# One fused attention and expert kernel: scores of 64 queries as tiled float32 products, issued together with values

## The chip, the cores and the metric

The kernel runs on one core of one Trainium2 chip. The time is device microseconds from launch to end, as the median of some runs. Before the change three runs gave 751.17, 751.94 and 752.6 us, so the median is 751.94 us.

TensorE is called PE in the profile, VectorE DVE, ScalarE ACT, GpSimd POOL, and SyncE (here the engine that issues all loads and stores) SP.

## The reference

Input is q, k and v of 4 batches, 8 heads, 768 positions and 64 elements, and two weight matrices. Each query attends to its neighbours less than 16 positions away and to 24 summaries of 32 positions each; the summaries are a maximum over keys and a mean over values. Then a gated layer of width 2048 follows on the 3072 tokens of 512 elements.

```
k_sum = k.reshape(B, H, nb, block, D).max(axis=3)      # nb = 24, block = 32
v_sum = v.reshape(B, H, nb, block, D).mean(axis=3)
scores_l = scale * q @ k^T, kept where |i - j| < 16
scores_s = scale * q @ k_sum^T + log(32)
a = softmax over both; attn = a @ [v, v_sum]
h = x @ w_in;  g = h - tanh(h);  out = g @ w_out
```

## The kernel before

**Units.** The work is cut into 8 units `u`, each half of a batch's positions (384 queries) with all 8 heads. Attention of a unit goes by 4 pairs of heads `p` and 3 tiles of 128 queries `i`. The gated layer of a unit (called MoE in the code) goes by 16 steps `f`: products "in" into bank `pH`, activations, products "out" into the three banks `pY0` to `pY2`. The layer of unit u needs all four pairs of that unit, so attention of unit u+1 is run beside the layer of unit u, and only unit 0's attention stands alone at the start.

**Precision.** The first unit's layer takes whole float32 operands; the later ones take each operand as a high and a low part of a faster float32 kind (`F32R`) and add three products. The weights are read as raw words, and DVE and ACT turn each of the 32 weight tiles into numbers ("w scale", "w shift", "w low", "w sign"), later into a high and a low part.

**Scores before.** `prep` turns q and k with PE (`q turn`, `k turn`) and copies them out. k lies in a tile `[128, 2, KC]`: for each head of the pair its 64 rows, and zeros in the other 64. In units 0 and 1 (`u < WHOLE`) `scores` is one float32 product of 128 queries with 2 x 182 columns. From unit 2 on it is three `F32R` products with high and low parts, for which `prep` also makes `q low`, `q again`, `k low`, `k again`. 182 columns hold what 128 queries need; of these the first 64 queries use columns 0 to 117 and the last 64 use columns 64 to 181.

**Softmax before.** `softmax` works by tile. Because the two halves of 64 queries use other columns, `min` is run twice for each head, each on 64 partitions: it adds the mask and takes the minimum in one custom instruction, followed by a read of the accumulator. At the first and the last tile of a batch two memsets go before. Then per tile: two `exp` on ACT, `sum guard` and `inverse` on two sums, two `normal`. `transpose_probs` turns the probabilities with PE (`p turn`) and copies them out (`p out`), and `values` multiplies them with v: 12 float32 products for each pair, each of 64 columns into 64 partitions; in unit 0 they are issued tile by tile, from unit 1 on (`TOGETHER`) all 12 of a pair at once.

**Order.** Nothing runs in the order written. `plan.add` collects tasks with a cost in us, `Plan.schedule` chooses the task with the highest level at each moment, engine by engine, and the resulting order is what each engine executes, in order. `BIAS` adds to the level of single tasks, `KB` and `HALF` to that of a kind of task in one of three phases, `SL` says when an optional engine may take a task, and `keep_warm` fills PE's planned pauses before 100 us with products of the unit matrix (they appear as pX<-ident). All DMAs go through SP, in order, at most eight in flight.

Of the kernel before, what the change touches and what calls it, by code (L numbers as in the profile page):

```python
# [10 lines left out]
F32 = mybir.dt.float32  # L11
# [8 lines left out]
SLOTS = 4  # L20
# [7 lines left out]
TOGETHER = 1  # L28

WHOLE_IN = True  # L30
WHOLE_F = set(range(16))

WHOLE = 2

BIAS = {('top turn', 6): -62, ('p out', 19): -34, ('series', 46): -24, ('out', 95): 14, ('sum guard', 39): 21, ('p turn', 21): 39, ('q turn', 8): 13, ('square', 3): 43, ('w load', 29): 33, ('exp', 139): 10, ('x high', 7): 25, ('square', 16): -7, ('exp', 47): 33, ('square', 5): 41, ('series', 95): -20, ('in', 16): 12, ('square', 15): 11, ('w load', 26): 59, ('w load', 17): -20, ('values', 23): -12, ('w scale', 7): 30, ('sum guard', 45): 20, ('top turn', 4): 19, ('w load', 25): -45, ('w load', 23): 8, ('square', 13): 19, ('w sign', 2): 26, ('out', 13): -36, ('min', 142): 21, ('w load', 28): 24, ('series', 11): 5, ('normal', 25): -15, ('p out', 23): 32, ('pick', 8): 55, ('mean out', 3): 7, ('direct', 11): -29, ('w load', 15): -31, ('values', 20): 40, ('out', 14): -19, ('exp', 44): -17, ('square', 8): 4, ('w load', 27): 21, ('min', 39): 30, ('g', 9): -24, ('pick', 9): 4, ('inverse', 19): 36, ('direct', 8): -18, ('direct', 14): 20, ('q high', 8): 12, ('w high part', 21): -20, ('cube', 1): 21, ('normal', 44): -4, ('in', 8): 8, ('w sign', 10): -32, ('in', 1): 24, ('sum', 1): -20, ('x low', 7): -31, ('k load', 35): -9, ('tanh', 6): 20, ('v load', 39): -20, ('square', 9): 8, ('series', 15): -4, ('direct', 6): 1, ('v load', 90): 60, ('normal', 35): -15, ('values', 13): -30, ('exp', 37): -15, ('out', 58): 60, ('out', 67): -30, ('top put', 17): -5, ('k high', 3): 30, ('sum guard', 1): 60, ('top put', 80): 60, ('v load', 88): -45, ('g low', 56): -30, ('k load', 8): 60, ('k high', 36): -5, ('sum guard', 34): 15, ('out', 17): -5, ('mean put', 24): 5, ('sum guard', 2): -5, ('w low part 2', 22): -45, ('k again', 31): -15, ('k high', 12): -60, ('k load', 33): 30, ('inverse', 39): 5, ('min', 53): -15, ('tanh', 20): 30, ('out', 44): -30, ('y store', 23): 15, ('in', 13): 30, ('inverse', 88): -60, ('w low part 2', 24): 15, ('w sign', 18): 30, ('w low part 2', 4): -60, ('k high', 17): 60, ('k load', 37): 5, ('normal', 11): -15, ('chunk sum', 4): -60, ('top pre', 1): 60, ('top turn', 8): 30, ('x whole', 3): 5, ('scores', 37): 5, ('min', 165): 15, ('min', 23): 15, ('w shift', 6): 60, ('normal', 33): 30, ('w shift', 27): 60, ('w shift', 2): -30, ('chunk load', 11): 30, ('inverse', 4): -30, ('min', 46): -5, ('series', 9): -60, ('in', 21): 15, ('exp', 16): 15, ('normal', 70): -60, ('min', 6): -5, ('w low part 2', 20): -15, ('k turn', 4): 25, ('sum guard', 4): 60, ('q turn', 1): 30, ('out', 106): -5, ('in', 31): -5, ('g low', 96): 15, ('v load', 66): -5, ('top put', 52): -15, ('values', 9): 15, ('w high part 2', 29): -30, ('normal', 49): -30, ('chunk load', 3): 5, ('mean put', 11): 30, ('scores', 0): 30, ('g high', 26): -15, ('in', 30): 60, ('out', 38): -15, ('g high', 15): 60, ('q low', 3): -5, ('in', 12): 5, ('v load', 68): -60, ('w scale', 21): 15, ('p turn', 38): -45, ('out', 98): 15, ('k load', 25): 30, ('sum guard', 44): -30, ('g high', 99): -5, ('top put', 26): -30, ('w load', 4): 60, ('tanh', 71): -5, ('v load', 41): -5, ('w shift', 5): 30, ('v load', 141): 30, ('top put', 3): -5, ('q load', 8): 30, ('out', 89): -15, ('k load', 40): -30, ('v load', 43): 30, ('exp', 51): -60, ('w shift', 26): 5, ('scores', 34): 30, ('mean turn', 1): -30, ('out', 55): 5, ('w scale', 10): -30, ('tanh', 5): -60, ('exp', 30): -5, ('top put', 19): 5, ('out', 163): -60, ('v load', 21): -5, ('g low', 19): 5, ('g high', 86): -15, ('w shift', 7): 30, ('q low', 31): -60, ('g', 18): -5, ('x whole', 2): 15, ('w high part 2', 19): -5, ('q load', 19): -60, ('sum', 7): -30, ('min', 112): 30, ('v load', 89): 15, ('k load', 31): -5, ('tanh', 37): -15, ('inverse', 41): 30, ('out', 83): -15, ('w sign', 21): 30, ('k load', 3): -60}

PREP = [0, 2, 6, 11]

TOPS = {0: [(0, 0)], 1: [(0, 2)], 3: [(0, 1)], 5: [(0, 3)], 9: [(1, 3)], 11: [(1, 2)], 13: [(1, 0)], 15: [(1, 1)]}
SUMS = {0: [(0, 0)], 1: [(0, 1), (1, 1)], 8: [(0, 2)], 9: [(0, 3)], 10: [(1, 0)], 11: [(1, 2)], 13: [(1, 3)]}  # L40

# [1128 lines left out]
```

## Time and profile before

| | |
|---|---|
| median of three runs | 751.94 us |
| profiled execution, span from the first to the last instruction | 749.3 us |
| PE busy | 716.6 us (96%) |
| DVE busy | 479.4 us (64%) |
| ACT busy | 488.7 us (65%) |
| POOL busy | 225.7 us (30%) |
| mean granted PE clock | 0.993 |

The span is one profiled execution; the runs' times hold 2.6 us more (751.94 against 749.3) that lie outside its first and last instruction. A float32 product shows as two records in the profile, an `F32R` product as one; so 12 products of values show as x24. A matmul's record overlaps the next one's, so what a matmul costs is read from one start to the next, not from its duration. All helper calls share one line (L70), so groups are told apart by tile names: `pS` scores, `pT` turned things, `pX` values, `prob` probabilities, `probT` turned ones, `stat` minima and sums, `wraw` raw weights, `wf` and `wh` weights, `vw` values of v, `rawq` and `rawk` loaded q and k.

### The profile page before, as it was taken

The page shows a single profiled execution, that of the slowest core. Times are in us where ns is not written, and L with a number is a line of the kernel's source. Part 1 is how long each engine was busy: PE and PEld are TensorE (multiplying, and loading weights), DVE is VectorE, ACT ScalarE, POOL GpSimd, SP SyncE. Part 2 cuts the span into 40 slices and gives each one's busy share as a digit, 9 for nine tenths or more (in the row PEclk, how much of TensorE's full clock was granted, in tenths as well). Part 3 has the DMA queues.
Part 4 walks back from the last instruction along what each step waited for, and adds up shares of the span by engine and source line. Part 5 has one row for each costly group of instructions (what it writes and reads, how often), then busy time and mean ns, then how long its engine had stood idle before and what let it go on. Part 6 is the DMA issues. An engine that isn't in the chain of part 4 may idle for free. (4 is left out here: it accounts for less than half of the span.)

```text
span 749.3 us, 13632 instructions
## 1 busy us (share of the span) xinstructions
PE 716.6 (96%) x4351; PEld 590.2 (79%) x4351; DVE 479.4 (64%) x1685; ACT 488.7 (65%) x1413; POOL 225.7 (30%) x314
## 2 busy tenths in 40 slices
PE   7878899999999999999999999999999999999995
PEld 5655544457888898878888898889888888888994
DVE  5878999897775468774766558754767377651111
ACT  4557887648765577767777667656757577755442
POOL 3001221425434325453222225423132223222221
PEclk9989999999999999999999999999999999999999
DMA  9877586433031031423112131302112130101001
GB/s 234 234 216 187 173 229 194 164 101 91 30 82 23 17 86 65 103 72 95 44 30 54 39 87 54 83 5 77 45 25 58 39 87 1 40 1 43 1 1 48
DMA packets 121522, 61.03 MB, mean 81 GB/s; under 512 B 92512, under 2 KB 113248, under 8 KB 121440
## 3 DMA queue, kind: packets, MB, share of 16 engines
q1 hardware_dynamic: 121440, 60.06, 29.6%
q8 instruction: 37, 0.61, 0.3%
q14 instruction: 45, 0.37, 0.1%
HBM read 51.38 MB, written 6.29 MB: 77 GB/s over the span
## 5 line engine op out<-in xcount | busy, mean ns | idle before, releaser
L70 PE MATMUL pH<-xh,wf 128*128 128x384 f32 x548 | 186.5, 374 | 3.4 <-DVE wf L70 1.9
L70 POOL TENSOR_TENSOR gv<-gu,gt 128x384 f32<-128x384 f32 x109 | 111.5, 1024 | 236.1 <-DVE gl L70 142.8
L70 PE MATMUL pY<-wf,gh 128*128 128x512 f32 x432 | 178.6, 440 | 0.0
L70 PE MATMUL pH<-xh,wh 128*128 128x384 f32 x448 | 155.9, 348 | 0.0
L70 PE MATMUL pH<-xl,wh 128*128 128x384 f32 x448 | 152.2, 340 | 0.0
L70 PE MATMUL pY<-wh,gh 128*128 128x512 f32 x336 | 140.9, 419 | 0.0
L70 ACT ACTIVATE gu<-pH 128x384 f32<-128x384 f32 x128 | 62.5, 488 | 114.0 <-PE pH L70 95.9
L70 PE MATMUL pY<-wh,gl 128*128 128x512 f32 x336 | 132.0, 393 | 0.0
L70 ACT ACTIVATE prob<-prob,stat 128x118 f32<-128x118 f32 x236 | 92.0, 392 | 56.8 <-DVE stat L70 50.0
L70 PEld LDWEIGHTS pH<-xh,wf 128*128 128x128 f32 x548 | 102.4, 189 | 25.5 <-ACT gt L70 3.2
L70 DVE CUSTOM_DVE_ANT_0 prob<-pS,mask 64x118 f32<-64x118 f32 x352 | 98.0, 278 | 34.5 <-PE pT L70 15.3
L70 DVE TENSOR_TENSOR gl<-gv,gh 128x384 fp32r<-128x384 f32 x76 | 44.0, 579 | 90.4 <-ACT gh L70 83.7
L70 PEld LDWEIGHTS pY<-wf,gh 128*128 128x128 f32 x432 | 80.3, 189 | 20.8 <-issue 11.0
L70 PEld LDWEIGHTS pH<-xh,wh 128*128 128x128 f32 x448 | 84.5, 189 | 3.2 <-ACT prob L70 0.2
L70 PEld LDWEIGHTS pH<-xl,wh 128*128 128x128 f32 x448 | 83.9, 187 | 0.0
L70 PEld LDWEIGHTS pY<-wh,gl 128*128 128x128 f32 x336 | 63.1, 188 | 14.7
L70 PEld LDWEIGHTS pY<-wh,gh 128*128 128x128 f32 x336 | 63.4, 189 | 9.6
L70 ACT ACTIVATE gu<-gu 128x384 f32<-128x384 f32 x128 | 66.9, 523 | 0.2
L70 ACT ACTIVATE gt<-pH 128x384 f32<-128x384 f32 x128 | 61.8, 483 | 0.3
L70 POOL TENSOR_TENSOR gl<-gv,gh 128x384 fp32r<-128x384 f32 x36 | 37.6, 1045 | 78.7 <-ACT gh L70 36.3
L70 PE MATMUL pS<-k,q 128*128 128x364 f32 (+1 forms) x176 | 46.0, 343 | 8.3 <-DVE stat L70 5.1
L70 DVE TENSOR_SCALAR prob<-prob,stat 128x118 f32<-128x118 f32 x133 | 47.7, 385 | 2.4
(151 smaller groups left out, 1028.6 us busy)
## 6 DMA issues: line engine op xcount, KB each, us to landing
wraw<-in_moe_w_in_dram SPq DMA_DIRECT2D x16, 512.0 KB
wraw<-in_moe_w_out_dram SPq DMA_DIRECT2D x16, 512.0 KB
rawq<-in_q_dram SPq DMA_DIRECT2D x48, 128.0 KB
out_dram<-tmp SPq DMA_DIRECT2D x24, 256.0 KB
rawk<-in_k_dram SPq DMA_DIRECT2D x32, 128.0 KB
vw<-in_v_dram SPq DMA_DIRECT2D x40, 96.0 KB
vw<-in_v_dram SPq DMA_DIRECT2D x48, 64.0 KB
wraw<-in_k_dram SPq DMA_DIRECT2D x16, 192.0 KB
```

The costliest lines, as they stand in the source:

```text
L70: return lambda *args, **kwargs: self._tc.keep_in_program_order(op(*args, **kwargs))
```

## The change

**Scores.** q is now what gets the zeros: a tile `[128, 2, U]` in which head a has its 64 rows and zeros elsewhere, and k is a plain `[128, KC]` tile with both heads. A score product takes 64 queries of one head and the 118 columns that these need: 12 float32 products for each pair, in all units. The two halves of a tile go to different partitions (0 to 63 and 64 to 127) of the same columns of the bank, so that both use the same 118 columns. A pair's scores fill the two banks `pS0` and `pS1`. The low parts and second copies of q and k are gone.

**Together.** From unit 1 on the scores of a pair and the values of the pair before are one task (`scores_and_values`), so PE issues values and then scores without anything between.

**Softmax** is by pair: six `min` of 128 partitions, one for each tile and head, six `exp`, one guard and one inverse on six sums, six `normal`. The edge memsets became two further masks. `p turn` uses the banks `pX`, `pS0` and `pS1`; the banks `pS` and `pT` are now `pS0` and `pS1`.

**Tables.** `BIAS`, `SL`, `KB` and `HALF` are new, some costs and the planner's transfer rates changed, `tmp` has three buffers and the `qa` tile is gone.

```diff
-        if 2 * b < WHOLE:
-            to, n = top_bases(b, g)[0], NB * (p % PG)
...
+        to, n = top_base(b, g), NB * (p % PG)
...
-        either("q high", {ACT: 0.371, DVE: 0.465}, ..., r=[(pq, 0)], w=[(qh, n) for n in range(2)])
-        for a, x in enumerate(qs):
...
-            do("q low", DVE, 0.47, low, r=[(pq, 0), (qh, 0)], w=[(x, 1)])
-            either("q again", {DVE: 0.269, ACT: 0.413, POOL: 1.4}, ...
...
-                do("k low", DVE, 0.6, ...
...
-                either("k again", {DVE: 0.336, ACT: 0.5, POOL: 1.85}, again, ...
+        for a in range(2):
             rows = slice(64 * a, 64 * a + 64)
+            either("q high", {ACT: 0.38, DVE: 0.5}, lambda e, a=a, rows=rows: copy(e, at(qf)[rows, a], at(pq)[rows, :U], -1.0 / math.sqrt(D)), r=[(pq, 0)], w=[(qf, a)])
...
+        either("k high", {ACT: 0.52, DVE: 0.6}, lambda e: copy(e, runs(), at(pk).rearrange("p (r c) -> p r c", r=4)), r=[(pk, 0)], w=[(kf, 0)])
...
+    def score(u, p):
+        qf, kf = ("qf", p % 2), ("kf", p % 2)
+        for i in range(NT):
+            s, c = score_of(u, p, i)
+            for a in range(2):
+                for half in range(2):
+                    k0 = KS * i + 64 + 64 * half
+                    tensor.matmul(at(s)[64 * half:64 * half + 64, c + N2 * a:c + N2 * (a + 1)], at(qf)[:, a, P * i + 64 * half:P * i + 64 * half + 64], at(kf)[:, k0:k0 + N2], start=True, stop=True)
...
+    def scores_and_values(now, before, tags, px_tag):
+        r, w, cost, parts = [], [], 0.25, []
+        if before is not None:
+            px = bank(("px", *before), px_tag)
...
+            parts.append(lambda: value(*before))
+        if now is not None:
...
+            parts.append(lambda: score(*now))
+        do("scores" if now is not None else "values", PE, cost, lambda: [go() for go in parts], r=r, w=w)
+
+    def softmax(u, p):
+        st = buf(("st", u, p), "stat", [P, 12], F32, 3)
+
+        def first(i, a):
+            s, c = score_of(u, p, i)
+            c += N2 * a
+            m = 1 if u % 2 == 0 and i == 0 else 2 if u % 2 == 1 and i == NT - 1 else 0
+            vector.tensor_tensor_reduce(at(("pr", u, p, i))[:, a], at(s)[:, c:c + N2], mask[:, m], 1.0, 3e38, ALU.add, ALU.min, at(st)[:, 2 * i + a:2 * i + a + 1])
```

**What moves, first place: PE before the first product of the layer.** In unit 0 the layer can start when the values of its fourth pair are out. Here `wf` is a weight tile, `rawk` and `rawq` belong to unit 1's first pair, `gh`, `gt` and `gu` hold loaded keys for the summaries. Before:

```order
L70 MATMUL pX<-probT,vw 64x64 x4
L70 MATMUL pH<-ident,gh 128x128 x3
L70 MATMUL pH<-ident,gt 128x128 x3
L70 MATMUL pS<-k_112,q_187 128x364
L70 MATMUL pY_809<-probT,vw 64x64 x4
L70 MATMUL pX<-ident 128x128
L70 MATMUL pS<-k_112,q_187 128x364
L70 MATMUL pT<-ident,prob 118x128 x2
L70 MATMUL pH<-xh,wf_598 128x384 x4
```

Now:

```order
L68 MATMUL pY_787<-ident,prob 118x128 x2
L68 MATMUL pX<-ident,rawq 128x128 x3
L68 MATMUL pH<-ident,gh 128x128 x3
L68 MATMUL pY_803<-probT,vw 64x64 x12
L68 MATMUL pH<-ident,gt 128x128 x3
L68 MATMUL pS_824<-ident,rawk 128x128 x4
L68 MATMUL pH<-xh,wf_628 128x384 x4
L68 MATMUL pS_848<-k_198,q_149 64x118 x8
```

The first layer product came after three tiles of unit 1's scores, and now comes ahead of them, behind the turning of unit 1's first keys; the 12 value products of a pair, which stood in pieces of four or eight, stand in one row.

**Second place: SP, the loads around the first weights.** `wraw` is a raw weight tile, `gv` and `gl` are loaded values for the means. Before:

```order
L70 DMA rawk_109<-in_k_dram 15x4x64 [waits DMAHW7_49]
L70 DMA gt_749<-in_k_dram 128x3x128 [waits DMAHW0_49]
L70 DMA gu_761<-in_k_dram 128x3x128 [waits DMAHW1_49]
L70 DMA gh_770<-in_k_dram 128x3x128 [waits DMAHW2_49,DVE_49]
L70 DMA vw_110<-in_v_dram 96x4x64 [waits DMAHW3_49]
L70 DMA vw_110<-in_v_dram 64x4x64 [waits DMAHW4_49]
L70 DMA vw_110<-in_v_dram 32x4x64 [waits DMAHW5_49]
L70 DMA gh_803<-in_k_dram 128x3x128 [waits DMAHW6_49]
L70 DMA wraw_815<-in_moe_w_out_dram 128x1024 [waits DMAHW7_49,DVE_49]
L70 DMA wraw_822<-in_moe_w_in_dram 128x4x256 [waits DMAHW0_49,DVE_49]
```

Now:

```order
L68 DMA rawk_109<-in_k_dram 15x4x64 [waits DMAHW1_49]
L68 DMA rawk_109<-in_k_dram 128x4x64 [waits DMAHW2_49]
L68 DMA rawk_109<-in_k_dram 128x4x64 [waits DMAHW3_49]
L68 DMA rawk_109<-in_k_dram 64x4x64 [waits DMAHW4_49]
L68 DMA wraw_751<-in_moe_w_out_dram 128x1024 [waits DMAHW5_49]
L68 DMA wraw_770<-in_moe_w_in_dram 128x4x256 [waits DMAHW6_49]
L68 DMA wraw_783<-in_moe_w_out_dram 128x1024 [waits DMAHW7_49,DVE_49]
```

Counted from the start, each repeat for itself, the last load of unit 1's keys that the first layer product now stands behind (64x4x64) is SP's 77th transfer. The values of unit 0's second group of heads end with the 59th and its means with the 64th; before, the values ended with the 78th (the last vw row here) and the means with the 69th. The first tile of w_in is the 50th (48th before), the first of w_out the 78th (51st before), the second of w_in the 79th (66th before).

**Third place: DVE, the minima of unit 0's second pair.** `ISA` is the minimum with its mask, or the read of its accumulator. Before, its first tile:

```order
L70 MEMSET pY0_341 64x15
L70 ISA prob_395,stat_396<-pY0_341,mask_70 64x118
L70 ISA stat_396 64x1
L70 ISA prob_395,stat_396<-pY0_341,mask_70 64x118
L70 ISA stat_396 64x1
L70 MEMSET pY0_341 64x15
L70 ISA prob_395,stat_396<-pY0_341,mask_70 64x118
L70 ISA stat_396 64x1
L70 ISA prob_395,stat_396<-pY0_341,mask_70 64x118
L70 ISA stat_396 64x1
```

Now, the whole pair:

```order
L68 ISA prob_350,stat_351<-pY0_332,mask_70 128x118
L68 ISA stat_351 128x1
L68 ISA prob_367,stat_351<-pY0_332,mask_70 128x118
L68 ISA stat_351 128x1
L68 ISA prob_350,stat_351<-pY0_332,mask_70 128x118
L68 ISA stat_351 128x1
L68 ISA prob_381,stat_351<-pY1_341,mask_70 128x118
L68 ISA stat_351 128x1
L68 ISA prob_367,stat_351<-pY0_332,mask_70 128x118
L68 ISA stat_351 128x1
L68 ISA prob_381,stat_351<-pY1_341,mask_70 128x118
L68 ISA stat_351 128x1
```

Ten instructions for one tile became twelve for three.

More of the change, by code (lines that the diff above doesn't have):

```diff
@@ L326, in program @@
     WIN = 15
[L327 to L328 removed]
+    N2 = 64 + NB + 30
     KS = P + NB
@@ L783, in runs @@
-        def runs(j, a):
-            x = at(kx[j]).bitcast(dt)[64 * a:64 * a + 64, a, :]
-            return bass.AP(tensor=x.tensor, offset=x.offset, ap=[list(x.ap[0]), [KS, 4], [1, P]])
-        def keys(a):
-            return at(pk)[64 * a:64 * a + 64].rearrange("p (r c) -> p r c", r=4)
-        for a in range(2):
-            either("k high", {ACT: 0.478, DVE: 0.6}, lambda e, a=a: copy(e, runs(0, a), keys(a)), r=[(pk, 0)], w=[(kx[0], a)])
-            if len(kx) > 1:
-                do("k low", DVE, 0.6, lambda a=a: vector.tensor_tensor(runs(1, a), keys(a), runs(0, a).bitcast(F32), op=ALU.subtract), r=[(pk, 0), (kx[0], a)], w=[(kx[1], a)])
@@ L793, in prep @@
-        if len(kx) > 1:
-            for a in range(2):
-                def again(e, a=a):
-                    x = at(kx[0])
-                    copy(e, x[64 * (1 - a):64 * (1 - a) + 64, a, 64:], x[64 * a:64 * a + 64, a, 64:].bitcast(F32))
-                either("k again", {DVE: 0.336, ACT: 0.5, POOL: 1.85}, again, r=[(kx[0], a), (kx[0], "sums%d" % a)], w=[(kx[0], "zero%d" % a)])
-    def prep_sums(u, p):
-        _, kx = operands(u, p)
-        tops, keys, cols = top_of[u // 2, p]
-        def put(e, j, a):
-            rows = slice(64 * a, 64 * a + 64)
-            x = at(kx[j]).bitcast(F32)[rows, a, P:]
-            to = bass.AP(tensor=x.tensor, offset=x.offset, ap=[list(x.ap[0]), [KS, NT], [1, NB]])
-            if u >= WHOLE:
-                to = to.bitcast(F32R)
-            copy(e, to, at(tops[j])[rows, cols[a]:cols[a] + NB].bitcast(F32).unsqueeze(1).broadcast_to([64, NT, NB]))
-        for a in range(2):
-            for j in range(len(kx)):
-                either("top put", {POOL: 0.36, DVE: 0.14, ACT: 0.153}, lambda e, j=j, a=a: put(e, j, a), r=[keys[j]], w=[(kx[j], "sums%d" % a)])
@@ L1044, in program @@
         convert(i)
-    top_pair(0, 0, "pT")
+    top_pair(0, 0, "pH")
+    pairs = [(u, p) for u in range(NU) for p in range(NP)]
+    early_banks = {0: ("pS0", "pS1", "pX"), 1: ("pY0", "pY1", "pY2")}
     for j in range(NS + LAG + 3):
@@ L1069, in program @@
             load_qk(*divmod(j // (PG * SLOTS) + 1, NG))
-        if early and s0[2] >= 0:
-            scores(*s0, tag_s)
-        s = tile_slot(j - 1)
-        if s is not None:
-            softmax(*s)
+        if s0 is not None and c == 1:
+            softmax(u, p)
         if m2 is not None:
```

284 lines of the change are left out of this document (118 added, 166 removed).

## The prediction

> **What bounds the kernel now.** I read the page first (span, busy shares, the slices), then the busy times by stage, then PE's waits, then single rows of PE, DVE and SP.
>
> ```profile
> span 749.3 us, 13632 instructions
> ...
> PE 716.6 (96%) x4351; PEld 590.2 (79%) x4351; DVE 479.4 (64%) x1685; ACT 488.7 (65%) x1413; POOL 225.7 (30%) x314
> ...
> PE   7878899999999999999999999999999999999995
> ...
> PEclk9989999999999999999999999999999999999999
> DMA  9877586433031031423112131302112130101001
> ```
>
> PE is full from the sixth slice on; only the start has holes. The stages, cut at the first layer product (60 us), at the end of unit 0's layer (160 us) and at the last product (743 us):
>
> ```profile
> core 0: us, PE busy (x) PEld busy (x) DVE busy (x) ACT busy (x) POOL busy (x), PEclk, DMA share, GB/s
> 0.00:60.00 60.00, 47.55 (x467) 35.08 (x468) 42.52 (x213) 33.12 (x108) 7.44 (x31) 0.94 0.89 227
> 60.00:160.00 100.00, 92.04 (x376) 48.93 (x375) 92.23 (x246) 74.25 (x190) 25.64 (x35) 1.00 0.60 178
> 160.00:743.00 583.00, 577.07 (x3510) 506.14 (x3510) 344.70 (x1228) 380.74 (x1114) 192.67 (x249) 1.00 0.19 50
> ```
>
> Three stages with three limits. Up to 60 us DMA (0.89) and DVE (42.5 of 60) carry the work and PE idles 12.4 us, apart from its filling products. From 60 to 160 us PE and DVE are both busy 92%, and PE idles 8.0 us. After that PE alone is the bound: it idles 5.9 of 583 us, and DVE has 238 us to spare. What PE waited for, from 60 to 160 us (the first four) and after 160 us (the last three):
>
> ```profile
> PE pH L70 <- DVE wf L70: 1.9, 4, 1.0
> PE pS L70 <- DVE k L70: 1.8, 1, 1.8
> PE pH L70 <- ACT gt L70: 1.5, 2, 0.8
> PE pS L70 <- DVE stat L70: 1.0, 1, 1.0
> ...
> PE pS L70 <- DVE stat L70: 3.1, 7, 0.7
> PE pS L70 <- DVE k L70: 2.0, 2, 1.8
> PE pT L70 <- DVE qa L70: 0.8, 1, 0.8
> ```
>
> Mostly DVE. So a change that frees DVE pays before 160 us, and hardly after; there PE's own work has to shrink.
>
> **PE's work.** Scores of a tile from unit 2 on, scores in units 0 and 1, values of a pair (24 records are 12 products), and a short piece of values:
>
> ```profile
> 404.79 0.41 PE L70 MATMUL pS<-k,q 128*128 128x364 f32 x2
> ...
> 405.16 0.38 PE L70 MATMUL pT<-ident,prob 128*118 128x128 f32 x2
> ...
> 415.60 0.40 PE L70 MATMUL pY<-wh,gl 128*128 128x512 f32 x1
> 415.93 0.92 PE L70 MATMUL pX<-probT,vw 118*64 118x64 f32 x24
> 416.78 0.50 PE L70 MATMUL pY<-wh,gh 128*128 128x512 f32 x1
> 417.11 0.40 PE L70 MATMUL pY<-wf,gh 128*128 128x512 f32 x1
> ...
> 85.23 0.78 PE L70 MATMUL pS<-k,q 128*128 128x364 f32 x2
> 85.84 0.38 PE L70 MATMUL pT<-ident,prob 128*118 128x128 f32 x2
> ...
> 32.36 0.45 PE L70 MATMUL pY<-probT,vw 118*64 118x64 f32 x8
> ```
>
> From start to start, an `F32R` score tile takes 405.16 - 404.79 = 0.37 us, 0.39 with what it costs the neighbours, and a float32 one 85.84 - 85.23 = 0.61. Three make a pair: 1.17 and 1.83 us. The values: the layer product at 415.60 and the one at 416.78 usually take 0.23 us to the next start. From 415.60 to 417.11 are 1.51 us, less 0.46, so the block costs 1.05 us.
>
> What is in it: 24 records last 0.92 us and 8 last 0.45, so one more record is 0.47 / 16 = 0.029 us, 24 are 0.71, and 0.35 us is paid once per block for going into 64-column products and back. A float32 record of 364 columns takes 0.61 / 2 = 0.305, so 64 columns alone would be 0.054 us. At 0.029 two records run at once, one for each half of the partitions.
>
> The new scores are built in the same way, with 118 columns: 24 records of 118/64 x 0.029 = 0.054 us, or 1.30 us at most; by pure streaming (0.305 x 118/364 / 2 = 0.049) 1.19. I take 1.25. A joined block is then 0.35 + 0.71 + 1.25 = 2.31 us. From unit 2 on (24 pairs) it replaces 1.17 + 1.05 = 2.22, so +0.09 x 24 = **+2.2 us**. In unit 1 (4 pairs) it replaces 1.83 + 1.05 = 2.88, so -0.57 x 4 = **-2.3 us**. Bounds of the two together: -1.5 to +1.3. Float32 instead of three faster products costs PE nothing net, and gains it nothing.
>
> The Trainium skill, "TensorEngine Tiling", section Key Properties, says that changing the tiling mode drains TensorE. The 0.35 us beside 0.71 of streaming agree; turned tiles of full width show no such surplus. By that rule scores apart from values would pay 0.35 again, 28 x 0.35 = 10 us, which joining them avoids.
>
> **DVE's work.** One minimum of 64 partitions, what there is of them up to 60 us, and the small ones:
>
> ```profile
> 12.15 0.27 DVE L70 CUSTOM_DVE_ANT_0 prob<-pY,mask 64x118 f32<-64x118 f32 x1
> ...
> 12.46 0.28 DVE L70 CUSTOM_DVE_ANT_0 prob<-pY,mask 64x118 f32<-64x118 f32 x1
> ...
> L70 DVE CUSTOM_DVE_ANT_0 prob<-pY,mask 64x118 f32<-64x118 f32 x32 | 8.9, 278 | 1.0
> L70 DVE CUSTOM_DVE_ANT_0 prob<-pS,mask 64x118 f32<-64x118 f32 x24 | 6.7, 279 | 1.3 <-PE pY L70 0.5 <-PE pS L70 0.4
> L70 DVE RECIPROCAL stat<-stat 128x2 f32<-128x2 f32 x13 | 2.1, 163 | 0.3
> L70 DVE TENSOR_SCALAR stat<-stat 128x2 f32<-128x2 f32 x12 | 2.0, 163 | 0.1
> ...
> L70 DVE TENSOR_TENSOR k<-pS,k 64x512 fp32r<-64x512 f32 x48 | 33.1, 689 | 0.7
> ```
>
> A minimum with its read takes 0.31 us from start to start. The operation streams 118 elements in either case, so I price the one of 128 partitions the same. Up to 60 us 56 become 28 (-8.7 us), and 25 guards and inverses become 9 or 10 (-2.4 us): about -11 of 42.5 us. From 60 to 160 us the other 40 of units 0 and 1 become 20: -6 us, and -3 with guards. After 160 us the lows and copies of q and k go as well (the last row, `k low`, is 33.1 us of DVE alone), all hidden behind PE there: no gain by itself, but "DVE k" and "DVE qa" (2.8 us) have nothing left to wait for. The two further masks on POOL are hidden: POOL is busy 7.4 of the first 60 us and the first minimum starts at 12.15.
>
> **The start.** When can the layer begin?
>
> ```profile
> 43.10 1.78 SPq L70 DMA_DIRECT2D vw<-mean  x2
> ...
> 49.28 1.82 SPq L70 DMA_DIRECT2D vw<-in_v_dram  x3
> ...
> 51.68 0.43 SPq L70 DMA_DIRECT2D wraw<-in_moe_w_out_dram  x1
> ...
> 48.81 1.03 PE L70 MATMUL pX<-probT,vw 118*64 118x64 f32 x16 [0.78 <-DMA vw<-mean]
> ...
> 60.31 1.13 PE L70 MATMUL pH<-xh,wf 128*128 128x384 f32 x3
> ```
>
> In the new order unit 0's values and means are SP's 59th and 64th transfers, not the 78th and 69th, so they no longer hold the start. But PE has to turn unit 1's keys ahead of the first layer product, and their last load is the 77th. The 77th of before lies in the piece at 49.28, at about 49.8. The means issued from 43.10 to 44.88 were in use at 48.81, 3.9 us after the last issue. So 49.8 + 3.9 + 0.4 for the turn gives a first product at about 54.2 in place of 60.3: **-6 us**. Bounds: 0 if the transfers come later or the weights do, -11 if all of DVE's saving comes through. The next weights cover it: the first tile of w_out and the second of w_in are the 78th and 79th, right behind the keys, issued at 50 to 52, landed by 56 and converted by 58, when the first product (2.7 us) and unit 1's first scores (1.6 us) are through. If they are later, PE stands still and the gain is lost.
>
> **The second stage.** PE idles 8.0 us there; 4.7 us of the rows above are DVE's. DVE loses 9 of its 92 us, so I take **-3 us**, between -6 and +3 (late weights). **After 160 us** the waits on DVE total 5.9 us; I take **-2**, between -5 and, with the rival below, +15.
>
> Sum: 749.3 - 6 - 3 + (2.2 - 2.3) - 2 = 738.2 us of span. The runs' median lies 2.6 us above the span: **741 us**.
>
> **Rivals.**
>
> *The transfers hold the start.* For: DMA is busy 0.89 up to 60 us and the same bytes have to come. Against: they come in another order, with the weights last. Then only the second stage pays, -1 to -4 in all: 748 to 751 us.
>
> *The pair's loop comes late (slower).* Before, three tiles followed one another through two banks. Now a pair's scores, minima, exponentials, turning and copies have to be through before the next joined block, which holds the old values and the new scores, and everything behind it on PE waits too. In PE's new order the turning of probabilities often follows the scores by some 25 layer products, 5 to 6 us. What lies between: a minimum 0.3, six exponentials, guard and inverse:
>
> ```profile
> 299.67 0.38 ACT L70 ACTIVATE prob<-prob,stat 128x118 f32<-128x118 f32 x1
> ...
> 300.05 0.38 ACT L70 ACTIVATE prob<-prob,stat 128x118 f32<-128x118 f32 x1
> ...
> 314.98 0.17 DVE L70 TENSOR_SCALAR stat<-stat 128x2 f32<-128x2 f32 x1 [0.55 <-ACT prob L70]
> ```
>
> At 0.38 us six take 2.3 us. With the first minimum, 0.55 for ACT's sums to reach DVE (as here), two small operations and a multiplication of 0.2 each, and 0.3 at two more handovers (an estimate between the 0.1 from one operation to the next on one engine and this 0.55) it is 4.5 us. That fits. If ACT runs two or three other operations of 0.38 us or more ahead of it each time, the loop is 0.5 to 1 us late, 27 times: +13 to +27, which ends at 754 to 768. From 0.4 us a pair on it eats the whole gain.
>
> *The halves do not run side by side.* Each half uses all 128 rows, so a load of weights could hold the other half's products. Then a block has 24 x 0.10 = 2.4 us in place of 1.25, +1.15 x 28 = +32: about 773. The rows of values, with 118 rows, speak against it. The Trainium skill, "TensorE: Matmul & The Clock Gate", Part 3, says that weight loads overlap running matmuls only for other row groups. That would give this rival; the 0.029 us per record in this trace does not agree.
>
> *More than forecast.* The start gains 10, and the second stage's waits go: 731 to 735.
>
> **Chances.** Forecast (736 to 746) 0.55; transfers hold 0.19, of which 0.05 within 0.2%; late loop 0.14; no pairing 0.03; more 0.09. A run of this kernel can tell about 0.2% (1.5 us) from no change. Faster: 0.55 + 0.14 + 0.09 = 0.78, of which I give 0.04 to the unknown order: 0.74. Same 0.09, slower 0.17. The range takes the forecast, most of "transfers hold" and part of "more": 733 to 751.
>
> **What would show it.** First layer product between 52 and 57 us, not 60; a joined block of 48 records lasting about 2.2 us from start to start, with score records 0.05 apart; minima of 128x118 at 0.28; PE idle under 6 us from there to the end of unit 0's layer; PE waiting on DVE k and qa gone. Wrong if PE waits on ACT exponentials or on turned probabilities appear again and again after 160 us, if the first weights are waited for at the start, or if score records are 0.1 us apart.

## The result, and the profile after

The changed kernel takes 727.1 us (median of four runs, 725.67 to 733.4) against 751.97 us of the kernel before on the same chip: ratio 0.969, 95% interval 0.964 to 0.974, 24.9 us faster. The forecast was 741 us with a range down to 733, so the direction was right and the gain was more than twice what was forecast. The profiled execution has a span of 723.9 us, 25.4 less than before. Each run here lies about 1.8 us above its own span (725.67 against 723.9), so of the 2.6 us that the forecast adds to the span some 0.8 are not time outside it: the profiled execution was a fast one.

The first view is the busy time by stage, with the cuts at the first layer product, at the first product with `xl` (unit 1's layer begins) and at the last one. From unit 1 on `xh` and `xl` are the high and low part of the layer's input, `wh` and `wl` those of its weights, `gh` and `gl` those of its activations; `wf` is a weight tile too. Of the changed kernel:

```profile
core 0: us, PE busy (x) PEld busy (x) DVE busy (x) ACT busy (x) POOL busy (x), PEclk, DMA share, GB/s
0.00:54.50 54.50, 41.57 (x550) 36.31 (x551) 24.36 (x110) 27.23 (x94) 6.64 (x32) 0.97 0.86 216
54.50:150.10 95.60, 94.27 (x489) 53.07 (x488) 87.23 (x215) 71.87 (x202) 23.24 (x31) 1.00 0.70 204
150.10:705.00 554.90, 554.79 (x3791) 490.90 (x3790) 139.15 (x517) 337.72 (x1036) 253.35 (x323) 1.00 0.20 52
705.00:723.90 18.90, 11.65 (x52) 9.13 (x50) 0.56 (x2) 5.16 (x11) 6.02 (x6) 0.88 0.13 47
```

And of the kernel before, cut at the same events:

```profile
60.30:160.70 100.40, 92.44 (x379) 49.42 (x378) 92.63 (x246) 74.24 (x190) 26.34 (x35) 1.00 0.60 178
160.70:733.00 572.30, 567.58 (x3468) 498.68 (x3468) 342.31 (x1223) 377.11 (x1106) 190.96 (x248) 1.00 0.19 50
733.00:749.30 16.30, 8.78 (x39) 6.76 (x38) 1.68 (x4) 4.23 (x9) 1.01 (x1) 0.90 0.15 54
```

The start is 5.8 us shorter, the second stage 4.8, the long third stage 17.4, and the tail 2.6 longer (16 products "out" moved behind the last `xl` product, 3.7 us of work). The forecast had -6 for the start, -5.3 for the second stage (-3 and unit 1's -2.3), and +0.2 for all behind it. So the miss lies in the third stage, in which PE was "full" before.

The announced signs, in the timeline of PE: the first layer product, and a joined block between products of the layer. Columns are start, duration, engine, line, operation, tiles.

```profile
54.48 1.78 PE L68 MATMUL pH<-xh,wf 128*128 128x384 f32 x5
...
434.00 0.40 PE L68 MATMUL pY<-wh,gl 128*128 128x512 f32 x1
434.33 0.92 PE L68 MATMUL pX<-probT,vw 118*64 118x64 f32 x24
435.08 1.38 PE L68 MATMUL pS<-k,q 128*64 128x118 f32 x24
436.39 0.50 PE L68 MATMUL pY<-wh,gh 128*128 128x512 f32 x1
436.73 0.40 PE L68 MATMUL pY<-wf,gh 128*128 128x512 f32 x1
```

From 434.00 to 436.73 are 2.73 us, less 0.47 for the two layer products: the block costs 2.26 us (forecast 2.31). From unit 1's layer on the score records start in pairs, two within 0.01 us and the next two 0.101 us behind them (median). That is 0.0505 us for each, half of what one record of 118 columns would need by the prediction's 0.305 us for 364, so the halves do run side by side.

What the idle column of PE doesn't tell is found by starts. For each group of instructions that interrupts the layer's products I took the time from the start of the product ahead to the start of the second product behind it, less the usual distance of those two products. The shortest of each kind is its work; what others of the same kind take above that is waiting. Waits between two products of the layer, with nothing between them, are not in this count; in these two kernels none is above 0.4 us. From the first to the last `xl` product:

| kernel | blocks | work, us | waiting, us |
|---|---|---|---|
| before | 171 | 88.4 | 12.4 |
| changed | 112 | 89.6 | 1.6 |

So the third stage's -17.4 is about -10.8 of waiting, +1.2 of work, -3.7 that moved to the tail, and -4.8 from the layer's own "in" products, which follow one another every 173.4 ns where it was 177.2 (mean distance of two starts of "in" products, those of 0.25 us and more beside a block left out; there are 1344, and before 1267 of them have another product of the layer right behind: 1267 x 3.8 ns). That leaves 0.7 us unassigned. The forecast had -2 for the waiting and nothing for the slot.

One of those waits before the change, on PE and then on DVE at the same time:

```profile
330.88 0.40 PE L70 MATMUL pY<-wh,gl 128*128 128x512 f32 x1
332.06 0.41 PE L70 MATMUL pT<-ident,prob 128*118 128x128 f32 x2 [0.78 <-DVE qa L70]
```

```profile
328.80 1.06 DVE L70 TENSOR_REDUCE top<-wraw 96x64 f32<-96x512 f32 x1
329.90 0.22 DVE L70 TENSOR_TENSOR top<-top 96x64 f32<-96x64 f32 x1
330.15 0.62 DVE L70 COPY top<-top 96x64 f32<-96x64 f32 x1
330.78 0.55 DVE L70 SCALAR_TENSOR_TENSOR q<-pT,q 64x384 fp32r<-64x384 f32 x1
331.35 0.56 DVE L70 SCALAR_TENSOR_TENSOR qa<-pT,q 64x384 fp32r<-64x384 f32 x1
```

The layer product at 330.88 would be followed after 0.23 us; it is followed after 1.18. The column shows 0.78 of the 0.95 us, since the product's own record is drawn over the first 0.17. DVE, with plenty of time in this stage, is simply in the middle of a queue of 3 us when PE's order calls for its result. No minimum is in this queue. The three operations on `top` are one task of the plan, with 1.1 us (`chunk max`); they take 1.98 from 328.80 to 330.78.

The minima, DVE before and after the change (`DVE_READ_ACCUMULATOR2_ANT` is the read that belongs to each):

```profile
219.53 0.27 DVE L70 CUSTOM_DVE_ANT_0 prob<-pS,mask 64x118 f32<-64x118 f32 x1
219.73 0.07 DVE L70 DVE_READ_ACCUMULATOR2_ANT stat<- 64x1 f32 x1
219.82 0.28 DVE L70 CUSTOM_DVE_ANT_0 prob<-pS,mask 64x118 f32<-64x118 f32 x1
```

```profile
194.74 0.28 DVE L68 CUSTOM_DVE_ANT_0 prob<-pS,mask 128x118 f32<-128x118 f32 x1 [7.90 <-PE pS L68]
194.94 0.08 DVE L68 DVE_READ_ACCUMULATOR2_ANT stat<- 128x1 f32 x1
194.94 0.28 DVE L68 CUSTOM_DVE_ANT_0 prob<-pS,mask 128x118 f32<-128x118 f32 x1
195.14 0.09 DVE L68 DVE_READ_ACCUMULATOR2_ANT stat<- 128x1 f32 x1
```

One half took 0.29 from start to start, so the minimum of a tile and head took 0.6 us, while the plan had 0.39. One of 128 partitions takes 0.20, and the plan has 0.36. Before, the plan had it 0.2 us too short, 192 times; now 0.16 too long. That is the lead which the experiments follow. It is not the only price that was too low, as the queue above shows.

### The profile page after: what moved, and what is told of

Read it like the earlier page. It is cut to its first block, busy times and chain, and to the rows that moved or that the text cites. A ratio compares the mean times of both kernels' runs of the same rounds, so it can differ in the third digit from the quotient of the medians.

```text
span 723.9 us, 13669 instructions
## 1 busy us (share of the span) xinstructions
PE 702.3 (97%) x4875; PEld 589.4 (81%) x4875; DVE 251.3 (35%) x842; ACT 442.0 (61%) x1341; POOL 289.3 (40%) x391
## 4 chain that ended last, share of the span: by engine, by line
PE 84%; DMA 5%; ACT 3%; SPq 2%; DVE 2%; POOL 2%; issue 1%; POOLq 0%; DVEq 0%
PE pY L68 36%; PE pH L68 35%; PE pS L68 8%; PE pX L68 5%; SPq L68 2%; DMA wraw<-in_moe_w_out_dram 2%; ACT prob L68 1%; DVE tmp L68 1%; POOL wraw L68 1%; DMA wraw<-in_moe_w_in_dram 1%; DMA gl<-in_v_dram 1%; DMA rawk<-in_k_dram 1%; DMA vw<-in_v_dram 1%; DMA vw<-mean 1%; ACT gu L68 1%
## 5 line engine op out<-in xcount | busy, mean ns | idle before, releaser
L68 POOL TENSOR_TENSOR gl<-gv,gh 128x384 fp32r<-128x384 f32 x110 | 111.7, 1017 | 169.8 <-ACT gh L68 127.4
L68 PE MATMUL pH<-xh,wh 128*128 128x384 f32 x448 | 152.9, 341 | 0.0
L68 POOL TENSOR_TENSOR gv<-gu,gt 128x384 f32<-128x384 f32 x95 | 97.3, 1024 | 86.2 <-ACT gu L68 55.3
L68 PEld LDWEIGHTS pY<-wf,gh 128*128 128x128 f32 x432 | 80.5, 189 | 23.5 <-issue 12.1
L68 DVE CUSTOM_DVE_ANT_0 prob<-pS,mask 128x118 f32<-128x118 f32 x180 | 41.1, 275 | 149.3 <-PE pS L68 125.6
L68 ACT ACTIVATE gh<-gv 128x384 fp32r<-128x384 f32 x82 | 43.1, 525 | 44.5 <-PE pY L68 37.0
L68 DVE CAST gh<-gv 128x384 fp32r<-128x384 f32 x30 | 11.1, 370 | 135.8 <-PE pY L68 107.7
L68 PE MATMUL pS<-k,q 128*64 128x118 f32 x720 | 42.3, 267 | 0.3 <-ACT k L68 0.3
```

The costliest lines, as they stand in the source:

```text
L68: return lambda *args, **kwargs: self._tc.keep_in_program_order(op(*args, **kwargs))
```

## The experiments

Theories for the missed part: (1) the relief of DVE's load; (2) the plan's price: PE waits where the fixed order counts on work that takes longer than planned, whatever DVE's load; (3) the new order and tables, with fewer breaks in the layer's stream; (4) for the 4.8 us of "in" products, the placement of tiles in SBUF. Each time is a median; ratios are against runs of the kernel before beside it (751 to 752 us).

**The minima alone.** The changed kernel with halves again, and the kernel before without them; in both all else, order included, is kept.

```diff
-            vector.tensor_tensor_reduce(... [:, a], at(s)[:, c:c + N2], mask[:, m], ...)
+            for rows in (slice(0, 64), slice(64, P)):
+                vector.tensor_tensor_reduce(... [rows, a], at(s)[rows, c:c + N2], mask[rows, m], ...)
```

> The changed kernel with each minimum in two instructions of 64 partitions again, in the same order: 192 instructions of DVE more at 0.28 us (+53 us of DVE's 251), a pair's minima take 3.3 us where they took 1.65. Theory that the missed part of the gain comes from the relief of DVE (stalls of PE ahead of scores, turned probabilities and others went from about 9 to 2 us): 3 to 8 us come back, to 730 to 735, with PE waits on DVE in the groups. Rival, that it comes from the order (one joined block for each pair, fewer breaks in the layer's stream): under 1 us, 727 to 728.

```diff
-            for half in range(2):
-                rows, cs = slice(64 * half, 64 * half + 64), slice(64 * half, 64 * half + N2)
-                vector.tensor_tensor_reduce(at(pr)[rows, a], o[rows, cs], mask[rows], ...)
+            vector.tensor_tensor_reduce(at(pr)[:, a], o[:, 0:N2], mask, ...)
```

> The kernel before with one minimum of 128 partitions where there were two of 64, in the same order. It takes the first half's columns for all rows, so the probabilities of the second 64 queries of each tile are not those of the reference; nothing else is left out. DVE has 192 instructions less (-53 us of 479). Relief of DVE: PE's idle time in 60 to 160 us falls from 8 to about 4 us and the stalls ahead of scores after 160 us shrink, 5 to 9 us faster, 743 to 747. Rival (order): under 2 us, 750 to 752.

With halves the changed kernel takes 743.8 us (ratio 0.987, 0.983 to 0.992): 14 to 17 of the 25 us are gone (by the ratios, by the medians). The kernel before without them takes 738.4 us (0.985, 0.981 to 0.989): 11 to 13 of the 25 us are won. Both are more than expected. Stages of the changed kernel with halves, and what PE waited for in its third stage (us in total, times, longest):

```profile
54.40:158.00 103.60, 97.08 (x489) 53.80 (x488) 97.25 (x275) 72.84 (x202) 23.87 (x30) 0.98 0.65 190
158.00:722.40 564.40, 558.86 (x3792) 490.29 (x3791) 188.46 (x793) 345.52 (x1036) 252.11 (x324) 1.00 0.20 51
```

```profile
PE pX L68 <- DVE prob L68: 3.8, 5, 1.4
PE pH L68 <- ACT gt L68: 0.8, 3, 0.4
```

In the third stage DVE is busy 188 of 564 us, less than in the kernel before, and yet PE waits again: by starts 8.2 us where it was 1.6. In the kernel before without halves the waiting is 5.6 in place of 12.4, at the same order and the same blocks. So the minima are the largest single cause, and it is waiting that they cause. Why a DVE that is busy a third of the time is late is not told by this: taking the halves away takes both their load and their wrong price.

**The same load elsewhere.** Five copies of `xl` onto itself, 28 times, behind a step that nothing in the softmax depends on.

```diff
+        def low():
             vector.tensor_tensor(at(xl)[:, p], at(px)[:, :U], ..., op=ALU.subtract)
+            for n in range(5):
+                vector.tensor_copy(at(xl)[:, p], at(xl)[:, p])
```

> The changed kernel with five copies of xl onto itself behind each x low of units 1 to 7 (28 pairs, about 0.39 us each, +55 us of DVE), so DVE has as much more to do as with the minima in halves, but behind a step that is not on the chain from scores to turned probabilities. The planner's cost is left. Total load theory: as a_halves from unit 1 on, +8 to +12, 735 to 739. Theory of the chain (a minimum holds the bank and the exp): under 3 us, 727 to 730.

748.5 us (0.996, 0.994 to 0.999), 21 us slower than the changed kernel; the theory of the chain falls, and the theory of load had forecast 10 us less than this. Each instruction that DVE executes in order delays those behind it, and PE waits 11.6 us in the third stage (table below). But load, or load that the plan doesn't know?

**The load, with its price in the plan.** Only the planner's costs are changed, in three kernels: the last one's `x low`, the halves of the changed kernel, and the halves of the kernel before.

```diff
-        do("x low", DVE, 0.47, low, ...
+        do("x low", DVE, 2.42, low, ...
```

> As a_load (five copies behind each x low), with the planner's cost of x low at 2.42 us in place of 0.47, what the six instructions take in the trace from the first start to the next one's. True price: 728 to 736 where a_load took 748.5. Load: 745 to 750. Tables: 738 to 748.

```diff
-            do("min", DVE, 0.36, ...
+            do("min", DVE, 0.67, ...
```

> As a_halves (minima of the changed kernel in halves), with the planner's cost of a minimum at 0.67 us in place of 0.36, so that the plan knows what they take; the order is planned anew, with the changed kernel's tables. Theory of the true price (the stalls come from work that the plan takes for shorter than it is, not from DVE's load): 727 to 734 where a_halves took 743.8. Theory of the load: 740 to 746. Theory of the tables (any new order costs about 10 us): 736 to 746.

```diff
-            do("min", DVE, 0.62 if edge else 0.39, ...
+            do("min", DVE, 0.85 if edge else 0.62, ...
```

> The kernel before with the planner's cost of a minimum at 0.62 us (0.85 at an edge) in place of 0.39 and 0.62; instructions are the same, the order is planned anew. The trace has two halves with their reads at 0.62 us, so the plan took 0.23 us too little, 192 times. If the stalls come from a plan that puts scores and turned probabilities where DVE cannot be ready, 5 to 13 us are won, 739 to 747; if the tables, made for 0.39, matter more, 752 to 765.

| third stage | time, us | plan's price wrong: stage, waiting | plan's price right: stage, waiting | time, us |
|---|---|---|---|---|
| copies behind x low | 748.5 | 567.8, 11.6 | 552.8, 3.2 | 731.6 |
| changed, minima in halves | 743.8 | 564.4, 8.2 | 550.3, 1.5 | 737.8 |
| before (minima in halves) | 752.0 | 572.3, 12.4 | 564.4, 5.6 | 742.4 |

(Ratios of the right prices: 0.974, 0.972 to 0.976; 0.984, 0.980 to 0.987; 0.988, 0.985 to 0.992.) The third stage of the kernel with the copies, with the wrong price and with the right one, one row each, and of the kernel before with the right price:

```profile
160.80:728.60 567.80, 558.78 (x3792) 489.85 (x3791) 192.69 (x635) 337.31 (x1034) 253.20 (x321) 1.00 0.20 51
```

```profile
56.20:158.00 101.80, 98.47 (x496) 54.88 (x495) 93.14 (x228) 78.03 (x216) 27.44 (x30) 1.00 0.63 186
158.00:710.80 552.80, 551.94 (x3785) 489.28 (x3784) 185.14 (x619) 344.11 (x1051) 253.86 (x318) 1.00 0.20 52
```

```profile
160.70:725.10 564.40, 562.38 (x3468) 497.83 (x3467) 335.66 (x1190) 378.98 (x1113) 203.66 (x268) 1.00 0.20 52
```

PE's largest wait in the third stage, in the kernel with the copies with the wrong and with the right price, and its wait ahead of scores in the kernel before with the right price (it was 3.1 us, 7 times, in the prediction's rows):

```profile
PE pX L68 <- DVE prob L68: 5.1, 5, 1.5
...
PE pX L68 <- DVE prob L68: 0.9, 2, 0.5
...
PE pS L70 <- DVE stat L70: 0.2, 1, 0.2
```

With the copies the work on DVE is the same within a few us (192.7 and 185.1), and the stage is 15 us shorter. Not all of that is waiting: with the right price 8 records of unit 0's float32 "out" products, 0.43 us each, come ahead of the cut (10 in the kernel with halves). About 3.4 us moved so, 8.4 are the waiting in the table, and 2.9 are waits between two products of the layer. The 55 us of copies cost the whole kernel 4.5 us once the plan knows of them, 21 if not. So theory 2 holds in the third stage and theory 1 doesn't. What the right price doesn't give back is lost ahead of it: with halves in the plan, unit 1's layer begins at 166.4 us in place of 150.1, and by its total of 737.8 us this kernel fits the expectation's theory of the tables rather than that of the true price. Two causes offer themselves there, and no run separates them: DVE's load (97 to 100 us busy of the second stage in both kernels with halves), and tables that were made for another order. The second alone can cost 9 us, as a_dear below begins unit 1's layer at 159.1 us without an instruction more.

**A price too low or too high, with unchanged instructions.**

```diff
-            do("min", DVE, 0.36, ...
+            do("min", DVE, 0.13, ...     (a_cheap)
+            do("min", DVE, 0.59, ...     (a_dear)
```

> The changed kernel, instructions unchanged, with the planner's cost of a minimum at 0.13 us in place of 0.36, so 0.2 us below what it takes, as much as the kernel before had it too low. True price: stalls ahead of scores and turned probabilities come, +8 to +14, 735 to 741. Load: nothing, 726 to 729.

> The counterpart: the planner's cost of a minimum at 0.59 us, as much too high, so the plan leaves time that is not needed. True price: no stalls, 726 to 731. Theory of the tables: as much lost as by a_cheap, 735 to 741.

734.7 us (0.979, 0.977 to 0.981) and 731.6 us (0.974, 0.972 to 0.976). This pair is weak evidence. The expectation of the cheap one rested on 0.33 us for a minimum, and by the rows above it is 0.20, so the plan was only 0.07 too low; its waiting is 2.6 us in the third stage (557.5 us long), with one more wait of 2.2 us between two products of the layer, and most of its loss lies in the second. The dear one has a third stage of 552.5 us, 2.4 shorter than the changed kernel, and begins it 9 us later; the 2.4 are no gain, as 8 such records of unit 0 come ahead of the cut there too. Each new order that I tried under the changed kernel's tables with its own minima costs 4 to 8 us, mostly before 160 us.

**The late stage of one and the early one of the other.**

```diff
+            do("min", DVE, 0.59 if u > 1 else 0.36, ...
```

> The changed kernel with the planner's cost of a minimum at 0.59 us from unit 2 on alone, 0.36 before. a_dear had this cost everywhere: 2.5 us shorter from the first to the last xl product (552.5 against 555.0), but 9 us later at the end of unit 0's layer (159.1 against 150.1). If the loss belongs to the early order and the gain to the later one, 724 to 726; if the stages can't be had apart, 728 to 732.

731.8 us (0.973, 0.970 to 0.977). Unit 1's layer begins at 154.1 us, the third stage takes 555.1 us: neither is had. No version that I ran is faster than the changed kernel.

**DVE relieved of the low parts, scores whole.** The kernel before with float32 scores of 364 columns in all units.

```diff
+SCORES = 8
-        if u < WHOLE:
+        if u < SCORES:
             return (("qf", p % 2),), (("kf", p % 2),)
```

> The kernel before with float32 scores of 128 queries and 364 columns in all units, as it has them in units 0 and 1; q low, q again, k low and k again go (about 80 us of DVE's 479, some of ACT's), minima stay in halves. The summaries of batches 1 to 3 enter the scores with their high parts alone. PE pays 0.66 us more for each of 24 pairs by the prediction's own prices (2.88 against 2.22), +16. If the relief of DVE counts wherever it comes from, at the rate of the minima (13 us for 53 us), 12 to 20 us come back: 748 to 756. If only the chain of the minima counts, 764 to 769.

769.2 us (1.025, 1.022 to 1.029). Work of the blocks rises from 88.4 to 106.1 us (+17.7; the prediction's prices give +16), waiting falls from 12.4 to 8.5 only, and a wait of 2.9 us between two products of the layer (at 169.5 us) is new, though DVE has 87 us less to do:

```profile
PE 735.2 (96%) x4279; PEld 590.1 (77%) x4279; DVE 392.8 (51%) x1535; ACT 456.5 (60%) x1335; POOL 222.4 (29%) x300
```

Taking more from DVE than the minima are does not buy what the minima buy, which speaks against theory 1. It does not single out theory 2: the low parts were priced too low as well, by about half as much for each as the minima (from start to start `q low` takes 0.58 us and `k low` 0.70, the plan has 0.47 and 0.6), and the order was planned anew. It also shows the arithmetic's part: float32 at 118 columns with two halves at once costs PE what three faster products of 182 columns cost, and at 364 columns it doesn't.

**Breaks in the stream.** Values and scores as two tasks.

```diff
             parts.append(lambda: value(*before))
+            if now is not None:
+                do("values 2", PE, 0.9, parts.pop(), r=r, w=w)
+                r, w, cost = [], [], 0.15
```

> The changed kernel with values and scores of units 1 to 7 as two tasks, values without an entry in the tables. Theory of breaks: each of 28 more breaks of the layer's stream costs what a product behind a break takes over the others (0.32 against 0.24 us), +2 to +4; with a change of tile form at each end of the added piece (0.35 us a block) up to +10: 730 to 737. Rival, that joining is worth nothing: 727 to 728.

739.1 us (0.985, 0.981 to 0.988). Scores alone and values alone, each between two layer products:

```profile
206.51 0.39 PE L68 MATMUL pY<-wh,gl 128*128 128x512 f32 x1
206.83 1.43 PE L68 MATMUL pS<-k,q 128*64 128x118 f32 x24
208.19 0.50 PE L68 MATMUL pY<-wh,gh 128*128 128x512 f32 x1
208.53 0.39 PE L68 MATMUL pY<-wf,gh 128*128 128x512 f32 x1
...
209.46 0.40 PE L68 MATMUL pY<-wh,gl 128*128 128x512 f32 x1
209.79 0.92 PE L68 MATMUL pX<-probT,vw 118*64 118x64 f32 x24
210.64 0.50 PE L68 MATMUL pY<-wh,gh 128*128 128x512 f32 x1
210.98 0.40 PE L68 MATMUL pY<-wf,gh 128*128 128x512 f32 x1
```

2.02 - 0.47 = 1.55 and 1.52 - 0.47 = 1.05 us: together 2.60 against 2.26 joined. Joining is worth 0.34 us a pair, 9.5 us for 28. In the third stage the work of the blocks rose by 7.4 us (89.6 to 97.0) with waiting at 1.5; the stage got only 4.0 longer, as other work moved ahead of it, where unit 1's layer began 9.8 us later. So this is a part of the change on its own, and the prediction had it inside its 2.31. It is not what was missed, since the work of the blocks came out as forecast.

A second try kept the order and let only the values of a pair follow behind the next layer product:

```diff
+        def go():
+            parts[-1]()
+            later.extend(parts[:-1])
...
+        if getattr(t, "kind", "") in ("in", "out"):
+            while later:
+                later.pop(0)()
```

> The changed kernel in the same order but for the 27 joined blocks: scores stay where they are, the values of the pair before follow behind the next product of the layer. So the layer's stream has 27 breaks more and nothing is planned anew. A product behind a break took 0.32 us where the others take 0.24, and before had 171 breaks where the changed kernel has 112. Theory of breaks: 27 times 0.08 to 0.35 us, +2 to +9, 729 to 736; a_split's loss from unit 1's layer on (+4.0) then is that, and its +8 ahead of it the new order. Rival, breaks cost nothing and the smaller count is only another way to write the stalls: under 1 us.

759.8 us (1.012, 1.009 to 1.015), and the time tells nothing of breaks: where a group's last values came behind the loads of the next group's v, they waited for these loads and used the wrong group's v.

```profile
PE pX L68 <- DMA vw<-in_v_dram: 6.9, 3, 2.6
```

The work of its blocks, which leaves waits out, does tell: 97.2 us in 135 blocks against 89.6 in 112, 0.33 us for each block more, as in the first try.

**The tables.** Both kernels with `BIAS`, `SL`, `KB` and `HALF` empty.

```diff
-BIAS = {('const', 1): 103, ...
+BIAS = {}
```

> The changed kernel with its four tables (additions to the levels, limits of optional engines) empty, costs as they are. With the next kernel it tells what the tables are worth and how far the gain is theirs. Theory that the gain belongs to the work and its price: this kernel stands 20 to 35 us below the kernel before with its tables empty, whatever both lose; 745 to 775. Theory of the tables: the two are within 8 us.

> The kernel before with its four tables empty. Work and price: 775 to 810, 20 to 35 us above the changed kernel with empty tables. Tables: within 8 us of it.

746.1 us (0.994, 0.991 to 0.996) and 769.6 us (1.025, 1.022 to 1.028). Tables are worth 19 us to the changed kernel and 18 to the one before, and without them 23.5 us remain of 24.9. The second is below its expected 775 to 810 us; the distance between the two is as expected. So the total gain is not the tables'. Where it lies does depend on them: without tables both kernels begin the layer at 85 to 86 us, the second stage differs by 7.1 us and the third by 13.2. The start's gain is the new tables' own. The other costs and the transfer rates that the change gave the planner are in both comparisons, and no run separates them.

**Placement.** 32 bytes unused between the high weights and all that lies behind them (`x`, low weights), in both kernels; and the changed kernel with everything 32 or 64 bytes lower. Instructions and order are unchanged.

```diff
+    fixed(("pad",), [P, 8])
     fixed(("mean",), [P, HG * D])
```

> The kernel before with 32 unused bytes per partition ahead of everything that lies behind the high weights in SBUF; order and instructions are the same. From the first to the last xl product the layer's 'in' products followed one another every 177.0 ns before and every 173.4 ns after the change (1344 of them, -4.8 us), whatever else ran. Theory of placement: it is where xh, xl and the low weights lie; here they lie a multiple of 64 bytes plus 32 away, as after the change, so the slot falls to about 173.4 ns and the time by about 5 us, to 747. Rival, that the slot belongs to the order or the neighbours: 177.0 ns and 752 us stay, within 0.5 us.

> The changed kernel with the same shift of 32 bytes for all that lies behind the high weights (two small constants moved into the tile of a third to make room); order and instructions are the same. Placement: the slot of 'in' products rises from 173.4 to about 177 ns and the time by 5 us, to 732. Rival: 173.4 ns and 727 us stay.

> The changed kernel with every tile from the sums on 32 bytes lower in SBUF (two constants moved into another tile); order and instructions are the same. The slot of 'in' products was 173.4 ns after the change, 175.1 ns with all but the high weights 32 bytes lower, 177.2 ns before and 175.6 ns before with the rest 32 bytes higher. If the offset of high weights against xh is what matters, 173.4 ns and 727 us stay; if the offset modulo 64 bytes of either, 175 to 177 ns and 729 to 732 us.

> The same with 64 bytes lower, so every offset modulo 64 bytes is that of the changed kernel. If modulo 64 bytes decides, the slot is 173.4 ns at each of the twelve places of a step, 727 us. If the whole address does, another pattern over the twelve places, with a mean between 170 and 178 ns and 723 to 732 us.

| kernel | mean distance of "in" products | time, us | ratio |
|---|---|---|---|
| before | 177.2 ns | 752.0 | |
| before, 32 bytes between | 175.6 ns | 749.9 | 0.998 (0.996 to 1.000) |
| changed | 173.4 ns | 727.1 | 0.969 (0.964 to 0.974) |
| changed, 32 bytes between | 175.1 ns | 728.2 | 0.969 (0.965 to 0.972) |
| changed, all 32 bytes lower | 173.4 ns | 727.2 | 0.967 (0.965 to 0.970) |
| changed, all 64 bytes lower | 173.4 ns | 727.6 | 0.968 (0.966 to 0.970) |

Twelve products of a step, first and last, before and after the change (the starts are 1.96 and 1.91 us apart):

```profile
423.34 0.37 PE L70 MATMUL pH<-xh,wh 128*128 128x384 f32 x1
...
425.30 0.34 PE L70 MATMUL pH<-xl,wh 128*128 128x384 f32 x1
```

```profile
443.46 0.34 PE L68 MATMUL pH<-xh,wh 128*128 128x384 f32 x1
...
445.37 0.34 PE L68 MATMUL pH<-xl,wh 128*128 128x384 f32 x1
```

Moving everything together changes nothing: the medians at the twelve places of a step stay within 1 ns, 169 to 178 ns in the same pattern. Moving `x` and the low weights against the high weights changes the pattern and the mean, by 1.6 ns both ways. So the place of the high weights in SBUF against the tiles behind them counts, and part of the 4.8 us is shown to be placement; that it is the distance between a product's two operands, and that placement is all of it, is only argued. The other kernels of the changed family in this document, placed as it is, have 173.4 to 173.9 ns, those of the other 175.5 to 177.2 (the lowest without tables), so the order of work moves it by more than 1 ns too. In the runs' times these 2 us can hardly be seen.

## Why the prediction was wrong, point by point

- **The start, -6.** 60.31 to 54.48 us in the profiled executions, forecast 54.2. Other executions of the same instructions (the shifted kernels) began at 55.4 to 57.5, so a typical gain is 3 to 6. It is the new tables', as the kernels without tables show. Transfers in another order fit as the cause, but no run changes them alone, and the path that I had named is not what ended last. PE's last idle time there, 0.92 us for `gl` (values for the means), ends at 49.37 us; from then on PE shows no idle time up to the layer, and the turn of unit 1's keys, whose last load was issued at 49.27, follows at 54.04 in PE's regular pace. That the first product came so near to 54.2 is partly luck.
- **The joined block, 2.31 us.** 2.26. The work of all blocks of the third stage went from 88.4 to 89.6, +1.2 where +2.2 was forecast. Right. That joining avoids 10 us of draining was right too: 28 x 0.34 = 9.5 us. By the Trainium skill, "TensorEngine Tiling (Array Packing)", section Key Properties, the change of tiling mode drains the engine; these rows agree, with 0.34 us more where one stretch becomes two.
- **The second stage, -3, with -2.3 for unit 1.** -4.8 in all. The size was right, the way was not quite: I had DVE lose 9 of its 92 us there, but from 60 to 160 us it is as busy as before (91.6 us), with other work drawn forward, and PE idles 1.3 us in place of 8.0. That DVE's load counts by itself in this stage is likely from these 91.6 of 100 us, but no run shows it apart from the order.
- **"After 160 us ... I take -2."** This step failed; the measured term is -10.8. Two readings were behind it. I took PE's waits from its idle column, 5.9 us. By the starts PE lost 12.4 us, nearly all of it in 34 blocks, since 0.17 us of each wait lie under the record of the product ahead. And I took DVE's 238 free us to mean that "a change that frees DVE pays before 160 us, and hardly after". PE follows a fixed order, and each result has a due time in it. The plan that set these had 0.39 us for a minimum of 0.6; the difference was in the sources, one cost in the code beside the 0.31 for each half that I had worked out. That price accounts for 6.8 of the 10.8 us: with it put right the kernel before waits 5.6 us, and as much with the halves taken away. The other 4.0 stay unassigned; other prices were too low too, of which no run tells what they cost. Pricing the new minimum at 0.31, as the old half, was too high as well: it is 0.20.
- **The layer's own products, nothing.** -4.8, at least partly from the placement of tiles, which no row of the profile before could tell.
- **Transfers hold the start** (748 to 751): no, as above. **The halves do not run side by side** (773): no, score records are 0.0505 us apart; the rule of the Trainium skill, "TensorE: Matmul & The Clock Gate", Part 3, that weight loads overlap running matmuls only for other row groups does not agree with these halves, which use all 128 rows. **The pair's loop comes late** (754 to 768): not in the changed kernel, whose waiting is 1.6 us. (The terms of its loop add up to about 4.35 us, not 4.5.) But its price was real: with the minima in halves, 2.4 us more for a pair (six times 0.6 - 0.2), the waits named there appear ("pX <- DVE prob") and more than half of the gain is eaten. **More than forecast** (731 to 735) came nearest, with too little, and for a reason that I had not given it.

## What to carry to other kernels

Where a planner fixes the order of each engine, the question on a change is not only how much work goes from which engine, but also whether the plan's price of each piece is the one in the trace: 55 us of work on an engine that is idle two thirds of the time cost 4.5 us with its price in the plan and 21 without. Compare those prices with the trace before anything else; the kernel before won 9 us by one number. And read waits of a pipelined engine from one start to the next, not from the idle column, which hid half of them here.

## What the runs showed of the hardware that I had not expected

- A minimum of 128 partitions with its read takes 0.20 us from start to start in a row, one of 64 partitions 0.29 to 0.32, so two halves cost three times the whole. With full partitions the next operation starts together with the read of the last (194.94 in the rows above), with halves 0.09 us behind it (219.73 and 219.82). Why, no run tells.
- 32 bytes between the high weights and the tiles behind them in SBUF change the distance of the layer's products from 173.4 to 175.1 ns in one kernel and from 177.2 to 175.6 in the other; 32 or 64 bytes under all of them change nothing.
- Float32 products of the form 128*64 (all 128 rows, 64 output partitions) run two at a time: 0.101 us for two records of 118 columns, and 2.26 us for a block of 24 of these and 24 of values. Each stretch of such products between others costs 0.34 us once.
